# Attention by chunks: the scan of the next decays ahead of the masked copies, and the decayed state copied by ScalarE

## The chip, the cores and the metric

The kernel runs on one core of a Trainium2 chip. The metric is the device time of one execution in microseconds, lower is better. The engines are TensorE (PE in the profile; PEld is its weight load), VectorE (DVE), ScalarE (ACT), GpSimd (POOL) and SyncE (SP), which issues most DMAs. Each works through its own instructions in order and waits on semaphores for the others.

## The reference

Three parts follow one another: a recurrent attention over 4 batches, 8 heads, 768 positions and a head size of 48; a mixture of 8 experts of which each token takes the best (a true gather and scatter); and a layer that takes the largest of three products. The attention, which is all that matters here:

```python
for t in range(S):
    kt, vt, rt, wt = (k[:, :, t], v[:, :, t], r[:, :, t], w[:, :, t])
    cur = np.einsum('bhd,bhe->bhde', u[None] * kt, vt)
    y[:, :, t] = np.einsum('bhd,bhde->bhe', rt, state + cur)
    state = wt[:, :, :, None] * state + np.einsum('bhd,bhe->bhde', kt, vt)
```

A state of 48x48 per batch and head decays by w at each position and takes up the product of k and v; each output reads the state before the update, plus a bonus term with u.

## The kernel before

The 768 positions of a batch are cut in 6 chunks of 128 (CH), so there are 24 chunks (NG), and the 8 heads are held as 4 pairs (NP), one head of a pair on partitions 0 to 47 and the other on 64 to 111. Within a chunk the recurrence is written as products of matrices: two scans along the positions on DVE make the running products of the decays, one backwards (gs, L324) and one forwards (es, L337). gs scales the transposed k (kS, L330) and es the transposed r (rt, L348), both read from PSUM.

- gram (L356) multiplies kS and rt to the scores, in two PSUM banks A. causal (L362) copies them under a mask into the tile AT, which diagonal (L309, POOL) has filled with the bonus on the diagonal and zeros elsewhere. These are the masked copies, two per chunk.
- kback (L372) turns kS back, update (L384) multiplies it by v to U. carry (L396, or L394 in a batch's first chunk) adds U to the decayed state: S. Then it multiplies S by the whole decay of the next chunk, pend, three times on POOL: twice into the two diagonal blocks of shat (L400, 48 partitions each), which the next chunk's outputs read, and once into the state that the next carry adds to (Sm, L403, in the first four chunks of a batch).
- outputs (L410 with shat, L417 with AT) makes y transposed, yT (L419) copies it out of PSUM, tokens (L426) turns it and multiplies by the expert embeddings; logits (L437, dot) sums those.
- bonus (z, L288, POOL) multiplies the transposed k and r; bonus_sum (L294) and bonus_turn (L302, c on ACT in L304) sum it with u; c is what diagonal spreads.
- transpose (L275) makes transposed w, k and r through two PSUM buffers T, taken in turn; ACT copies them out (L277, L282).

The order of all engines is written out by hand, in one loop over i (L608 to L694) with a software pipeline: an iteration works on the tokens of chunk i, the scores of g = i + 1, the bonus of j = i + 2 and the scans of h = i + 3. Small operations of the routing on DVE stand in a list, fillers, from which fill() takes one at a time at places in the code (among others between the two masked copies, after gs and after kS); the rest is taken at the end of the iteration. The routing works on groups of three chunks: in one iteration the fillers m, e, e, mx, oh (L458 to L466), in the next cum three times and the rest of the slot (L491 to L503), whose tail ohb and pay (L507, L495) comes at the end of that iteration; the third has few.

Behind the loop and partly inside its last two iterations, the first expert starts early: POOL issues the gather of its tokens (L842, from iteration 21 on), early_x turns them (L857), ACT and POOL split its weights (L826, L828), and early_h (L877) multiplies. Then come the experts and the wide layer, which the change doesn't touch.

The order of an iteration around the change:

```python
if ok(i): carry(i)
...
if ok(g): gram(g)
...
if ok(g): causal(g)
if ok(h): transpose(h, "k")
if ok(j):
    bonus_turn(j)
    diagonal(j)
if ok(h): scan(h)
if 0 <= i < NG - 1: outputs(i)
```

Of the kernel before, what the change touches and what calls it, by code (L numbers as in the profile page):

```python
# [7 lines left out]
F32 = mybir.dt.float32  # L8
# [17 lines left out]
CH = S // P  # L26
# [20 lines left out]
class Block:  # L47
# [64 lines left out]
    def attention(self):  # L112
# [3 lines left out]
        with ExitStack() as es:  # L116
# [199 lines left out]
                act.activation(out=junk, in_=wb[g % NW][:, :, :D], func=AF.Relu, bias=neg1,  # L316
                               accum_out=viol[:, g:g + 1])

            def scan(g):


                j, x = g % 2, st[g]
                gs = wp.tile([112, NP, P + 1], F32, tag="gs", name="gs", bufs=2)
                dve.tensor_tensor_scan(out=flat(gs)[:, ::-1], data0=wz[j][:, :0:-1], data1=flat(dG)[:, ::-1],  # L324
                                       initial=0.0, op0=ALU.mult, op1=ALU.max)
                dve.reciprocal(out=dE[:, :, 0:1], in_=gs[:, :, 0:1])
                act.activation(out=pend[:, g, :].unsqueeze(2), in_=gs[:, :, 0:1], func=AF.Copy)
                fill()
                x["kS"] = wp.tile([112, 512], F32, tag="kS", name="kS", bufs=3)
                scaled = lambda: dve.tensor_tensor(out=x["kS"].rearrange("q (p t) -> q p t", p=NP),  # L330
                                                   in0=x["k"][:112].rearrange("q (p t) -> q p t", p=NP),
                                                   in1=gs[:, :, 1:], op=ALU.mult)
                if g > 0:
                    scaled()
                fill()
                es_ = wp.tile([112, NP, P + 1], F32, tag="es", name="es", bufs=1)
                dve.tensor_tensor_scan(out=flat(es_), data0=wz[j][:, :-1], data1=flat(dE), initial=0.0,  # L337
                                       op0=ALU.mult, op1=ALU.add)
                x["es"] = es_
                if g == 0:  # L340
                    scaled()
                fill()
# [44 lines left out]
            def carry(g):  # L387
                b, c = divmod(g, CH)
                if c == CH - 1:
                    return  # L390
                sn = wp.tile([112, NP, D], F32, tag="S", name="S")
                u = st[g]["U"][:112, :192].rearrange("q (p e) -> q p e", p=NP)
                if c == 0:
                    dve.tensor_copy(sn, u)  # L394
                else:
                    dve.tensor_tensor(out=sn, in0=state[b], in1=u, op=ALU.add)  # L396
                j = (g + 1) % 2
                decay = lambda o, n: pend[o:o + n, g + 1, :].unsqueeze(2).to_broadcast([n, NP, D])
                for o in (0, 64):
                    pool.tensor_tensor(out=shat[j][o:o + D, :, o:o + D], in0=sn[o:o + D], in1=decay(o, D), op=ALU.mult)  # L400
                if c < CH - 2:
                    state[b] = wp.tile([112, NP, D], F32, tag="Sm", name="Sm", bufs=1)
                    pool.tensor_tensor(out=state[b], in0=sn, in1=decay(0, 112), op=ALU.mult)  # L403

            def outputs(g):
                c, j, x = g % CH, g % 2, st[g]
# [35 lines left out]
            def fill(n=1):  # L442
                while fillers and n:
                    fillers.pop(0)()
                    n -= 1
# [151 lines left out]
            with tc.manual_schedule():  # L597
# [10 lines left out]
                for i in range(-2, NG):  # L608
# [32 lines left out]
                    if i - 2 in ends and i < NG - 1:  # L641
                        route_rank(*ends[i - 2])
                        fillers.extend(route_slot(*ends[i - 2]))
                    if ok(g):
                        causal(g)
                    if ok(h):
                        transpose(h, "k")
                    if ok(j):
                        bonus_turn(j)
                        diagonal(j)  # L650
                    if ok(h):
                        scan(h)
                    if 0 <= i < NG - 1:
                        outputs(i)
                    if ok(g):
# [626 lines left out]
```

## Time and profile before

| what | us |
|---|---|
| median of 3 runs | 732.67 |
| lowest and highest of them | 732.01, 735.51 |
| the profiled execution's own time | 735.84 |
| its span, from the first to the last instruction | 734.1 |

The profile is of one execution. Its page gives the busy time of each engine over the span; the views that were asked of its trace give the same by stretch (windows), by line, or instruction by instruction (timeline). In a timeline row the first two numbers are the start and the duration in us; a bracket at the end is the time that the engine sat idle before, and what ended it. Operations on an engine overlap a little, since the next is started before the last has written everything. TensorE's granted clock is 1.00 of full speed throughout the loop's steady part, so a matmul's length means the same in all rows used here.

### The profile page before, as it was taken

The page shows a single profiled execution, that of the slowest core. Times are in us where ns is not written, and L with a number is a line of the kernel's source. Part 1 is how long each engine was busy: PE and PEld are TensorE (multiplying, and loading weights), DVE is VectorE, ACT ScalarE, POOL GpSimd, SP SyncE. Part 2 cuts the span into 40 slices and gives each one's busy share as a digit, 9 for nine tenths or more (in the row PEclk, how much of TensorE's full clock was granted, in tenths as well). Part 3 has the DMA queues.
Part 4 walks back from the last instruction along what each step waited for, and adds up shares of the span by engine and source line. Part 5 has one row for each costly group of instructions (what it writes and reads, how often), then busy time and mean ns, then how long its engine had stood idle before and what let it go on. Part 6 is the DMA issues. An engine that isn't in the chain of part 4 may idle for free.

```text
span 734.1 us, 13455 instructions
## 1 busy us (share of the span) xinstructions
PE 706.5 (96%) x4861; PEld 631.3 (86%) x4861; DVE 431.8 (59%) x938; ACT 308.0 (42%) x720; POOL 251.4 (34%) x271
## 2 busy tenths in 40 slices
PE   8999999999799999999999999999999999999994
PEld 5888888878689999999999988988988988889884
DVE  7899999999747887878788368522032031221120
ACT  4767666675435544555556322222121222221120
POOL 6666656566522402201100023443333333222222
PEclk7999999999979999999999999999999999999997
DMA  9997878843355537556564202000000100000001
GB/s 154 160 160 142 134 138 133 150 86 114 105 174 156 164 116 238 178 162 184 177 173 130 76 23 65 12 33 1 33 12 0 44 1 11 33 1 21 22 2 46
DMA packets 146444, 69.05 MB, mean 94 GB/s; under 512 B 104967, under 2 KB 140931, under 8 KB 146360
## 3 DMA queue, kind: packets, MB, share of 16 engines
q1 hardware_dynamic: 141752, 58.27, 34.7%
q0 software_dynamic: 4032, 9.74, 4.2%
q8 instruction: 42, 0.69, 0.4%
q14 instruction: 42, 0.34, 0.2%
q10 hardware_dynamic: 576, 0.01, 0.0%
HBM read 58.52 MB, written 9.48 MB: 93 GB/s over the span
## 4 chain that ended last, share of the span: by engine, by line
PE 83%; DVE 9%; DMA 3%; issue 2%; ACT 1%; POOL 1%; SPq 0%; POOLq 0%; DVEq 0%
PE psy L994 15%; PE psT L994 15%; PE psy L934 14%; PE psh L917 14%; PE psh L1018 9%; PE psT L275 4%; PE psA L356 2%; PE psM L426 2%; PE psY L417 2%; DVE AT L362 2%; DVE gs L324 1%; PE psY L410 1%; PE psT L904 1%; DMA out_dram<-raw,idx 1%; PE psM L372 1%
## 5 line engine op out<-in xcount | busy, mean ns | idle before, releaser
L1000 DVE TENSOR_TENSOR xg<-psT,xg 128x512 f32<-128x512 f32 x18 | 12.4, 690 | 112.9 <-PE psT L994 112.9
L828 DVE TENSOR_TENSOR lw<-raw,hw 128x384 fp32r<-128x384 f32 x120 | 62.2, 551 | 17.8 <-ACT hw L826 17.5
L826 ACT ACTIVATE hw<-raw 128x384 fp32r<-128x384 f32 x123 | 60.6, 524 | 17.2 <-ACT hw L826 11.4
L1008 POOL TENSOR_TENSOR lw<-xg,hw 128x512 fp32r<-128x512 f32 x24 | 31.4, 1308 | 100.1 <-ACT hw L1007 100.1
L842 POOL DMA_INDIRECT xg<-xs_d,idxs x25 | 26.9, 1075 | 112.9 <-PE psT L904 44.3
L1007 ACT ACTIVATE hw<-xg 128x512 fp32r<-128x512 f32 x24 | 15.2, 633 | 97.0 <-DVE xg L1001 97.0
L1008 POOL TENSOR_TENSOR lh<-xg,hh 128x512 fp32r<-128x512 f32 x12 | 16.0, 1332 | 114.8 <-ACT hh L1007 114.8
L994 PE MATMUL psy<-yh,mh 128*128 128x512 f32 x162 | 46.7, 396 | 0.2 <-ACT ys L938 0.2
L994 PE MATMUL psT<-yh,ml 128*128 128x512 f32 x162 | 46.6, 396 | 0.0
L994 PE MATMUL psy<-yl,mh 128*128 128x512 f32 x162 | 46.6, 395 | 0.0
L994 PE MATMUL psT<-yl,mh 128*128 128x512 f32 x162 | 46.6, 396 | 0.0
L994 PE MATMUL psy<-yh,ml 128*128 128x512 f32 x162 | 46.6, 396 | 0.0
L994 PE MATMUL psT<-yh,mh 128*128 128x512 f32 x162 | 46.5, 395 | 0.0
L288 POOL TENSOR_TENSOR z<-kT,rT 112x512 f32<-112x512 f32 x24 | 37.7, 1573 | 25.0 <-ACT rT L282 25.0
L309 POOL TENSOR_SCALAR_AFFINE_SELECT AT<-c 128x1024 f32<-128x1024 f32 x24 | 34.9, 1456 | 24.1 <-ACT c L304 24.1
L917 PE MATMUL psh<-xh,lw 128*128 128x420 f32 (+7 forms) x183 | 43.2, 346 | 0.0
L923 DVE SCALAR_TENSOR_TENSOR lh<-psh,hh 128x420 fp32r<-128x420 f32 (+6 forms) x56 | 31.4, 560 | 19.8 <-ACT hh L922 19.7
L917 PE MATMUL psh<-xh,hw 128*128 128x420 f32 (+7 forms) x177 | 42.6, 349 | 0.0
L917 PE MATMUL psh<-xl,hw 128*128 128x420 f32 (+7 forms) x177 | 41.3, 342 | 0.0
L1034 POOL DMA_INDIRECT out_dram<-raw,idx x24 | 23.7, 986 | 50.0 <-ACT raw L1024 27.7
L934 PE MATMUL psy<-hh,hw 128*128 128x420 f32 (+6 forms) x168 | 40.1, 344 | 0.0
L934 PE MATMUL psy<-lh,hw 128*128 128x420 f32 (+6 forms) x168 | 39.2, 341 | 0.0
(332 smaller groups left out, 1807.9 us busy)
## 6 DMA issues: line engine op xcount, KB each, us to landing
raw<-in_moe_w_dram SPq DMA_DIRECT2D x128, 192.0 KB, 3.1
raw<-in_moe_w_dram SPq DMA_DIRECT2D x18, 384.0 KB, 3.9
wb<-in_w_dram SPq DMA_DIRECT2D x24, 192.0 KB, 3.1
kb<-in_k_dram SPq DMA_DIRECT2D x24, 192.0 KB, 4.6
rb<-in_r_dram SPq DMA_DIRECT2D x24, 192.0 KB, 4.7
vb<-in_v_dram SPq DMA_DIRECT2D x24, 192.0 KB, 5.0
xs_d<-xt SPq DMA_DIRECT2D x24, 192.0 KB, 2.0
raw<-in_moe_w_out_dram SPq DMA_DIRECT2D x6, 384.0 KB, 4.8
```

The source lines that it names most:

```text
L275: pe.transpose(t[:112, p * P:(p + 1) * P], flat(src)[:, p * P:p * P + 112], ident)
L288: pool.tensor_tensor(out=x["z"], in0=x["kT"], in1=x["rT"], op=ALU.mult)
L309: pool.affine_select(out=x["AT"].rearrange("s q p t -> s (q p) t"), in_=x["c"].rearrange("t q p -> t (q p)").unsqueeze(2).to_broadcast([P, ...
L826: self.act.activation(out=hi, in_=raw, func=AF.Copy)
L828: eng.tensor_tensor(out=lo, in0=raw, in1=hi.bitcast(F32), op=ALU.subtract)
L842: self.pool.indirect_dma_start(out=t[:n], out_offset=None, in_=self.xs_d[0:rows], in_offset=bass.IndirectOffsetOnAxis(ap=self.idxs[:n, 4 * ...
L917: self.pe.matmul(t[:, c0:cap], a[:, d, :], b[:, d, c0:], start=(n == 0), stop=(n == 8))
L923: self.dve.scalar_tensor_tensor(out=lo, in0=t[:, c0:cap], scalar=0.0, in1=hi.bitcast(F32), op0=ALU.max, op1=ALU.subtract)
L934: self.pe.matmul(self.yb[m][:, :cap], a[:, m, :], b, start=(f == 0 and n == 0), stop=(f == 7 and n == 2))
L994: self.pe.matmul(t, a[:, d, f * P:(f + 1) * P], b[:, d, :], start=(n == 0), stop=(n == 8))
L1008: self.pool.tensor_tensor(out=lo, in0=c2, in1=hi.bitcast(F32), op=ALU.subtract)
L1018: self.pe.matmul(t[:, :DM], a[:, c], b[:, f, :], start=(n == 0), stop=(n == 17))
```

## The change

Two things change. The masked copies of chunk g are handed to the scan of chunk h, which issues them after its backward scan gs and the reciprocal, and before its fillers and kS; the forward scan es still follows kS. And carry makes the decayed state once, on POOL, in every chunk but a batch's last (in two buffers instead of one); a new function, spread, copies its two blocks into shat on ScalarE, after bonus_turn and diagonal in the iteration.

```diff
--- before.py
+++ after.py
@@ -316,7 +316,7 @@
                 act.activation(out=junk, in_=wb[g % NW][:, :, :D], func=AF.Relu, bias=neg1,
                                accum_out=viol[:, g:g + 1])
 
-            def scan(g):
+            def scan(g, between=lambda: None):
 
 
                 j, x = g % 2, st[g]
@@ -325,6 +325,7 @@
                                        initial=0.0, op0=ALU.mult, op1=ALU.max)
                 dve.reciprocal(out=dE[:, :, 0:1], in_=gs[:, :, 0:1])
                 act.activation(out=pend[:, g, :].unsqueeze(2), in_=gs[:, :, 0:1], func=AF.Copy)
+                between()
                 fill()
                 x["kS"] = wp.tile([112, 512], F32, tag="kS", name="kS", bufs=3)
                 scaled = lambda: dve.tensor_tensor(out=x["kS"].rearrange("q (p t) -> q p t", p=NP),
@@ -394,13 +395,16 @@
                     dve.tensor_copy(sn, u)
                 else:
                     dve.tensor_tensor(out=sn, in0=state[b], in1=u, op=ALU.add)
-                j = (g + 1) % 2
-                decay = lambda o, n: pend[o:o + n, g + 1, :].unsqueeze(2).to_broadcast([n, NP, D])
+                state[b] = wp.tile([112, NP, D], F32, tag="Sm", name="Sm", bufs=2)
+                pool.tensor_tensor(out=state[b], in0=sn, in1=pend[:, g + 1, :].unsqueeze(2).to_broadcast([112, NP, D]),
+                                   op=ALU.mult)
+
+            def spread(g):
+                b, c = divmod(g, CH)
+                if c == CH - 1:
+                    return
                 for o in (0, 64):
-                    pool.tensor_tensor(out=shat[j][o:o + D, :, o:o + D], in0=sn[o:o + D], in1=decay(o, D), op=ALU.mult)
-                if c < CH - 2:
-                    state[b] = wp.tile([112, NP, D], F32, tag="Sm", name="Sm", bufs=1)
-                    pool.tensor_tensor(out=state[b], in0=sn, in1=decay(0, 112), op=ALU.mult)
+                    act.activation(out=shat[(g + 1) % 2][o:o + D, :, o:o + D], in_=state[b][o:o + D], func=AF.Copy)
 
             def outputs(g):
                 c, j, x = g % CH, g % 2, st[g]
@@ -641,15 +645,18 @@
                     if i - 2 in ends and i < NG - 1:
                         route_rank(*ends[i - 2])
                         fillers.extend(route_slot(*ends[i - 2]))
-                    if ok(g):
-                        causal(g)
                     if ok(h):
                         transpose(h, "k")
                     if ok(j):
                         bonus_turn(j)
                         diagonal(j)
+                    if ok(i):
+                        spread(i)
+                    masked = (lambda: causal(g)) if ok(g) else (lambda: None)
                     if ok(h):
-                        scan(h)
+                        scan(h, masked)
+                    else:
+                        masked()
                     if 0 <= i < NG - 1:
                         outputs(i)
                     if ok(g):
```

## Rows read from the trace of the kernel before

**Rows 1.** Page, part 1: busy us (share of the span) and instructions of each engine.

```profile
PE 706.5 (96%) x4861; PEld 631.3 (86%) x4861; DVE 431.8 (59%) x938; ACT 308.0 (42%) x720; POOL 251.4 (34%) x271
```

**Rows 2.** View of windows, the scan loop: stretch, length, engines' busy us, PEclk, DMA, GB/s.

```profile
28.10:163.40 135.30, 128.70 (x1678) 113.87 (x1678) 126.29 (x269) 92.78 (x246) 83.56 (x104) 1.00 0.77 136
```

**Rows 3.** Timeline, gram starts of one cycle: start us, us, engine, line, operation.

```profile
112.80 1.16 PE L356 MATMUL psA<-rt,kS 48*128 48x128 f32 x16
...
127.87 1.16 PE L356 MATMUL psA<-rt,kS 48*128 48x128 f32 x16
...
134.62 1.16 PE L356 MATMUL psA<-rt,kS 48*128 48x128 f32 x16
...
149.58 1.16 PE L356 MATMUL psA<-rt,kS 48*128 48x128 f32 x16
...
156.18 1.16 PE L356 MATMUL psA<-rt,kS 48*128 48x128 f32 x16
```

**Rows 4.** Timeline, round D (134.62 to 141.78), all engines; idle before in brackets.

```profile
135.36 0.34 DVE L396 TENSOR_TENSOR S<-Sm,psM 112x192 f32<-112x192 f32 x1
...
135.88 0.74 DVE L362 COPY_PREDICATED AT<-msk,psA 128x512 f32<-128x512 int32 x1 [0.18 <-PE psA L356]
...
137.53 0.17 ACT L304 ACTIVATE c<-psM 128x8 f32<-128x8 f32 x1
...
137.55 1.22 DVE L324 TENSOR_TENSOR_SCAN gs<-wz,dG 112x516 f32<-112x516 f32 x1
...
137.83 1.83 POOL L309 TENSOR_SCALAR_AFFINE_SELECT AT<-c 128x1024 f32<-128x1024 f32 x1 [0.91 <-ACT c L304]
...
138.90 0.77 DVE L491 TENSOR_TENSOR cum<-cum,oh 128x8 bf16<-128x8 bf16 x1
...
138.98 0.60 ACT L419 ACTIVATE yT<-psY 112x512 f32<-112x512 f32 x1
...
139.60 0.68 DVE L330 TENSOR_TENSOR kS<-psT,gs 112x512 f32<-112x512 f32 x1
...
140.23 1.27 POOL L288 TENSOR_TENSOR z<-kT,rT 112x512 f32<-112x512 f32 x1 [0.57 <-ACT rT L282]
...
140.29 2.30 DVE L337 TENSOR_TENSOR_SCAN es<-wz,dE 112x516 f32<-112x516 f32 x1
...
140.33 0.65 PE L275 MATMUL psT<-ident,wb 128*112 128x128 f32 x4 [0.81 <-DVE kS L330]
```

**Rows 5.** Timeline, single rows of other rounds, all engines.

```profile
96.93 2.29 DVE L337 TENSOR_TENSOR_SCAN es<-wz,dE 112x516 f32<-112x516 f32 x1
...
144.66 0.18 DVE L437 TENSOR_REDUCE dot<-psM 128x8 f32<-128x32 f32 x1
...
145.10 1.09 POOL L309 TENSOR_SCALAR_AFFINE_SELECT AT<-c 128x1024 f32<-128x1024 f32 x1 [3.60 <-ACT c L304]
...
148.13 0.65 PE L275 MATMUL psT<-ident,wb 128*112 128x128 f32 x4 [0.60 <-DVE kS L330]
...
152.10 0.51 POOL L403 TENSOR_TENSOR Sm<-S,pend 112x192 f32<-112x192 f32 x1
...
152.91 1.77 POOL L309 TENSOR_SCALAR_AFFINE_SELECT AT<-c 128x1024 f32<-128x1024 f32 x1 [0.30 <-ACT c L304]
...
154.72 0.65 PE L275 MATMUL psT<-ident,wb 128*112 128x128 f32 x4 [0.49 <-DVE kS L330]
```

**Rows 6.** View of line L464 (the second e): count, duration ns min/median/max, starts.

```profile
L464 DVE TENSOR_TENSOR e<-e,w x9: 159/456/940, 45.1 to 189.3; 128x24 f32<-128x24 f32 x6, 128x16 f32<-128x16 f32 x3
```

**Rows 7.** Timeline, the last rounds: POOL and PE around the early gather.

```profile
173.14 1.08 POOL L400 TENSOR_TENSOR shat<-S,pend 48x192 f32<-48x192 f32 x2 [1.08 <-DVE S L396]
...
175.49 1.28 POOL L842 DMA_INDIRECT hw<-xs_d,idxs  x1 [0.69 <-issue]
...
181.26 0.55 PE L857 MATMUL psT<-ident,hw 128*128 128x128 f32 x3 [0.36 <-DMA hw<-xs_d,idxs]
```

**Rows 8.** View of line L241 (a copy by ScalarE in the set-up), durations in ns.

```profile
L241 ACT ACTIVATE sel<-ident x2: 351/355/359, 8.2 to 8.6; 48x192 f32<-48x192 f32 x2
```

## The prediction

> **What bounds the kernel now.** I read the page's busy shares first [rows 1]: TensorE (PE) 96%, VectorE (DVE) 59%. That hides two stages, so next I took the view of windows and cut the span at the end of the scan loop, the only stage the change touches. In it [rows 2] PE and DVE are both near 94% (128.70 and 126.29 of 135.30 us), ScalarE (ACT) at 69%, GpSimd (POOL) at 62%. Two engines nearly full, in order, each waiting for the other now and then: the most to be won is what each still waits.
>
> A round is the stretch from one gram (L356) to the next, and its starts in the timeline give the periods [rows 3]. Six rounds (one batch) make a cycle, which stands more than twice between 69 and 163 us, each round to within 0.1 us. I call its rounds A to F, with the cycle from 112.80 to 156.18: A and B together 15.07 us, C 6.75, D and E together 14.96, F 6.60, in all 43.38. In C the PE starts every matmul group as the one before lets go, so C cannot shrink by anything done to DVE. D, E and F would be shorter on PE alone: there PE waits for kS on DVE, 0.81, 0.60 and 0.49 us [rows 4, 5]. The tie is the PSUM buffer: the transposes of the next w (L275) need the one that kS (L330) reads last. So **what counts is when kS comes in A, D, E and F**, less when anything else does.
>
> Why is kS late? Take the timeline of D [rows 4]. The order on DVE is dot, S, then the masked copies (AT, L362), the scan gs, kS, the scan es. Two rows stand out. The third cum (L491) takes 0.77 us for 128x8, beside POOL's AT select, and kS follows only when that ends. And es takes 2.30, where gs, a scan of the same shape, takes 1.22: POOL's z started 0.06 us before it, and es ends about as long after z as a scan runs. The second e (L464) shows the same: 0.16 at the least, 0.46 in the median, where it stands beside Sm [rows 5, 6]. In the other direction POOL's AT select takes 1.83 beside gs and 1.09 alone [rows 4, 5]. So some DVE operations and POOL operations exclude each other, and the first to start keeps the other out. The masked copies and kS run at their usual length beside POOL.
>
> **The change, part by part.** *The order on DVE.* The same operations run, with gs and its reciprocal ahead of the two masked copies. In D, S starts at 135.36 and the next operation can follow 0.27 later. Now that is AT, which waits for gram until 135.88; after, gs starts at 135.63. Adding gs to kS without cum (1.26 to the reciprocal, 0.09 to the first copy, each as now), the copies come at 136.98 and 137.71 and the second cum at 138.33. POOL's AT select, which hangs on c (ScalarE, ending 137.70) as before, starts at 137.83 and is now alone: it ends at 138.92. The second cum waits for that, then the third, and kS starts at 139.15 instead of 139.60: 0.45 us sooner, and with it PE's w transposes, which have 0.81 to give.
>
> *es in D.* With kS at 139.15, es starts near 139.84, ahead of z at 140.23, which hangs on ACT and doesn't move. es then runs 1.22 and z waits: es ends 1.5 us sooner. The rest of D's work on DVE ends when z lets go, so dot of E comes not at 144.66 but near 143.45. Then all of E moves up by about 1.2 on DVE, to kS and the w transposes; PE can follow by the 0.45 it got in D and by the 0.60 it idles in E. **D and E: -1.05 us**; the bounds are -0.45 (z still first) and -1.4 (both idle times in full). It happens twice in the whole loop, the es at 96.93 us being the other one [rows 5]: -2.1. The first batch's D has no such es; between 0 and -0.45 I give it -0.15.
>
> *F.* S, m, then gs near 150.80, and the copies after it; the first e comes at about 152.79, just ahead of POOL's AT select at 152.91, which follows c [rows 5]. The second e, at 153.5, meets it and waits until 154.0, where before it waited for Sm only until 152.6. kS then starts 0.18 later than now and PE with it: **+0.18** three times, +0.55. In C the same delay fits in front of the w transposes: 0.
>
> *A and B.* A has the fillers of D, but its select starts later, with c behind one more matmul group, so its second cum waits longer; and B begins with DVE's backlog, which still ends when z does. Between 0 and D's -0.45 I take **-0.10** for the pair, three times, -0.3. The loop: -2.1 + 0.55 - 0.3 - 0.15 = -2.0 us.
>
> *POOL.* Per round two shat products of 0.5 go (1.08 the pair [rows 7]); one Sm stays, and is added in the fifth chunk of a batch, where there was none. Sm now meets gs, so it ends about 0.3 after gs (the AT select beside gs shows such a wait). Its reader in the next round is 4 us away: 0.
>
> *ScalarE.* Two copies of 48x192 per round, 0.355 each [rows 8], 0.71 in twenty rounds, on an engine with a third free. They stand after c and before pend and yT. In D c ends at 137.70; the copies end by 138.42, pend is free (gs ended at 136.9) and ends by 138.65, and yT began at 138.98 when its PSUM was full [rows 4]. Before, ACT stood idle there, held by pend for gs. So the cover is that idle time, and it is just enough: 0. If it were gone (Sm late), yT, its w partner on ACT and the tokens would slip by up to 0.4 a round. Behind the new wait for Sm stand pend and yT on ACT; outputs of the next round needs shat only 5 us later. The moved copies pass PE's k transposes, c and diagonal, none of which read AT's masked half; no DMA moves in the loop, and SP's loads hang on transposes, not on these.
>
> *The last rounds.* At 163.39 the round has F's fillers but starts late, so that the first e also meets the select: kS up to 0.8 later, of which es, which waits for the select now and not after, returns some. Between 0 and 0.8: +0.4. The gather of the early expert (L842) is behind shat, shat and Sm on POOL [rows 7]; after, behind Sm alone, 1.08 sooner. PE waits for its landing only 0.36 at 181.26, so of its 1.08 it can return 0.4 at most, which takes back the 0.4 just lost. Then POOL's eight low parts (L828) follow sooner, which is what DVE's second e (0.94 at its longest, 0.16 at its shortest [rows 6]) and two neighbours wait for. Bounds: 0, and -2.3 if all three wait as long, 0.78, and all of it goes. I take -0.7, nearly one of the three, as the low parts still overlap most of that stretch.
>
> Sum: -2.0 + 0.4 - 0.4 - 0.7 = **-2.7 us**, where the second 0.4 is what the gather's lead returns. The profiled execution took 735.84 with a span of 734.1; it becomes 733.1. Against the median of the runs shown, 732.67, which lies 3.2 under the profiled one: **730.0 us**.
>
> **Rivals.** *1. POOL starts first in C and F (slower).* The first e comes 0.12 before the select, gs 0.1 before Sm. If either tie falls the other way, e waits a whole select (1.09, from 152.91) or gs a whole Sm (0.51), and kS in both kinds of round comes 0.7 later: PE loses 0.7 in six rounds, +4.3, and the total is +1.6: **734.3**. For it: 0.12 us is near the spread of starts. Against: starts within a round repeat to 0.1 us from batch to batch. The Trainium skill, in "SBUF — State Buffer", section "Who interferes with whom", says that the one that issues first holds the shared port for its whole instruction, and that a vector operation with two SBUF inputs is of this kind; by that rule the second e and cum wait out the select as I have it, and a lost tie costs this full price.
>
> *2. Nothing comes of it.* If z is first in D after all, or the backlog's end isn't set by es, D and E give 0.45 twice and F takes 0.55, the rest 0: **732.3**. For it: PE is near full everywhere. Against: es at 2.30 occurs in both such rounds.
>
> *3. More.* All three late waits go (-2.3), D and E get 1.4 twice (-2.8), A gets D's 0.45 three times (-1.35) and F loses nothing: -6.4, **726.3**. For it: POOL has some 20 us less work in shat products. Against: the selects and low parts themselves remain, and something waits for them.
>
> *4. ScalarE is held.* If Sm waits beyond gs, for the copies too, ACT stands before pend and yT in nearly each round: 20 x 0.4 = 8 on top of -2.7: **738.0**. Against: the masked copies never lengthened beside POOL.
>
> **How the numbers follow.** Forecast 0.54, rival 1 0.17, rival 2 0.11, rival 3 0.13, rival 4 0.05. A measurement can tell about 0.5% from no change, 3.7 us: faster is under 729.0. The forecast's own range is 728 to 732.3, with over two fifths of its chance under 729.0; with rival 3 this makes faster 0.37, slower 0.06 (rival 4 and the end of rival 1), same 0.57. The range 726.0 to 735.0 reaches to rivals 3 and 1 and leaves out 4 and the ends.
>
> **What would show it.** Right: es never above 1.3 us beside z in D; kS 0.45 sooner there; periods of D and E together near 13.9 instead of 14.96, F 6.8, C still 6.75; no pend wait for gs on ACT; gather at about 174.5 less the loop's gain. Wrong: es again 2.3; a first e (L463) of 0.7 or more in C and F (rival 1); yT beginning well after its matmuls (rival 4); C shorter than 6.75, which would mean that PE wasn't its bound.

## The result and the profile after

The changed kernel takes **741.37 us** (median of 4 runs, 740.98 to 744.21); the kernel before, beside it, 733.97 (4 runs, 732.01 to 735.51). The ratio is 1.0081, 95% interval 1.0052 to 1.0111: slower, by some 6 us as the ratio has it (the medians lie 7.4 apart), where 730.0 was forecast. The profiled execution took 741.60 with a span of 739.9, against 735.84 and 734.1 before.

The trace falls into two halves of opposite sign. The first is the scan loop. The stretch that answers to [rows 2], from the loop's third gram to its third last, by the view of windows (stretch, length, busy us of PE, PEld, DVE, ACT and POOL, granted clock, DMA share, GB/s), for the changed kernel:

```profile
28.16:160.21 132.05, 127.72 (x1678) 113.85 (x1677) 123.16 (x269) 102.73 (x278) 71.47 (x75) 1.00 0.79 140
```

Between the same two grams (28.14 and 163.39 before) the loop takes 132.05 us where it took 135.25: 3.20 us less. ScalarE has 10 us more work in it and GpSimd 12 less. The gram starts of the cycle that answers to [rows 3], A to the next A, from the timeline:

```profile
111.24 0.94 PE L357 MATMUL psA<-rt,kS 48*128 48x128 f32 x12
...
126.13 1.16 PE L357 MATMUL psA<-rt,kS 48*128 48x128 f32 x16
132.88 1.16 PE L357 MATMUL psA<-rt,kS 48*128 48x128 f32 x16
...
146.43 1.16 PE L357 MATMUL psA<-rt,kS 48*128 48x128 f32 x16
153.20 1.16 PE L357 MATMUL psA<-rt,kS 48*128 48x128 f32 x16
```

A and B take 14.89 us (15.07 before), C 6.75 as before, D and E together 13.55 (14.96), F 6.77 (6.60). Round D itself, to be read against [rows 4]:

```profile
133.88 1.23 DVE L324 TENSOR_TENSOR_SCAN gs<-wz,dG 112x516 f32<-112x516 f32 x1
134.04 1.37 POOL L399 TENSOR_TENSOR Sm<-S,pend 112x192 f32<-112x192 f32 x1 [0.34 <-DVE S L397]
...
135.97 1.09 POOL L309 TENSOR_SCALAR_AFFINE_SELECT AT<-c 128x1024 f32<-128x1024 f32 x1 [0.56 <-ACT c L304]
...
137.19 0.68 DVE L331 TENSOR_TENSOR kS<-psT,gs 112x512 f32<-112x512 f32 x1
...
137.88 1.22 DVE L338 TENSOR_TENSOR_SCAN es<-wz,dE 112x516 f32<-112x516 f32 x1
...
137.93 0.65 PE L275 MATMUL psT<-ident,wb 128*112 128x128 f32 x4 [0.16 <-DVE kS L331]
138.55 1.62 POOL L288 TENSOR_TENSOR z<-kT,rT 112x512 f32<-112x512 f32 x1 [1.49 <-ACT rT L282]
```

The select takes its 1.09 us, es starts 0.67 ahead of z and takes 1.22 instead of 2.30, and TensorE waits 0.16 for kS where it waited 0.81. The last gram of the loop starts at 174.84 where it started at 177.68.

The second half is the end of the loop, up to the first expert's transposes: from that gram 23.81 us before (177.68 to 201.49), now 33.20 (174.84 to 208.04). The timeline of the changed kernel there, POOL, DVE and PE:

```profile
176.01 0.51 POOL L399 TENSOR_TENSOR Sm<-S,pend 112x192 f32<-112x192 f32 x1 [2.16 <-DVE m L462]
176.72 1.07 POOL L849 DMA_INDIRECT hw<-xs_d,idxs  x1 [0.21 <-issue]
...
177.48 7.08 DVE L468 TENSOR_TENSOR e<-e,w 128x16 f32<-128x16 f32 x1
177.82 1.02 POOL L835 TENSOR_TENSOR lw<-raw,lw 128x384 fp32r<-128x384 f32 x1
...
181.63 2.88 POOL L835 TENSOR_TENSOR oh<-raw,oh 128x384 fp32r<-128x384 f32 x3
...
185.02 0.17 PE L481 MATMUL psM<-oh,tri 128*128 128x8 bf16 x1 [6.47 <-DVE fl L537]
...
185.13 2.03 PE L414 MATMUL psT<-rt,shat 112*112 112x128 f32 x8
```

**The second e (now L468), 0.16 us at its shortest in [rows 6], takes 7.08.** It ends at 184.56, just when the last of GpSimd's seven low parts (now L835, ending 184.51) does. TensorE has nothing for 6.47 us, and its next outputs take 2.03 us instead of some 1.1. The windows of 5 us show why; first the changed kernel, then the kernel before:

```profile
175.00:180.00 5.00, 3.56 (x44) 3.04 (x45) 4.43 (x7) 4.76 (x13) 3.76 (x5) 1.00 0.85 253
180.00:185.00 5.00, 0.00 (x0) 0.00 (x0) 4.91 (x4) 0.96 (x3) 4.52 (x5) 0.61 0.12 36
185.00:190.00 5.00, 4.98 (x33) 4.35 (x33) 1.76 (x14) 0.60 (x1) 0.00 (x0) 0.50 0.02 3
190.00:195.00 5.00, 5.00 (x25) 5.00 (x25) 2.49 (x13) 2.24 (x7) 0.00 (x0) 0.50 0.11 41
195.00:200.00 5.00, 4.99 (x35) 4.62 (x33) 2.66 (x15) 1.97 (x6) 1.00 (x1) 0.69 0.51 157
```

```profile
180.00:185.00 5.00, 4.64 (x57) 3.97 (x54) 3.06 (x18) 3.55 (x9) 3.30 (x4) 1.00 0.57 171
...
190.00:195.00 5.00, 4.41 (x39) 4.02 (x38) 4.75 (x22) 1.36 (x5) 2.03 (x3) 1.00 0.24 78
```

After TensorE's idle stretch its granted clock is 0.50 (1.2 GHz) until 198 us, where before it stayed at 1.00 (2.4 GHz) to 201. Behind that both have one more stretch at 0.50: 201 to 211 before, 208 to 212 in the changed kernel. So the wait costs twice: once while it lasts, and once behind it.

Why did GpSimd have no such row before? There the second shat product of the last chunk waited for the landing of the early gather, and with it everything behind it on GpSimd. The timeline of the kernel before:

```profile
181.35 0.51 POOL L400 TENSOR_TENSOR shat<-S,pend 48x192 f32<-48x192 f32 x1 [1.95 <-DMA hw<-xs_d,idxs]
182.14 1.07 POOL L842 DMA_INDIRECT hw<-xs_d,idxs  x1 [0.28 <-POOL shat L400]
183.28 1.00 POOL L828 TENSOR_TENSOR lw<-raw,lw 128x384 fp32r<-128x384 f32 x1
```

By 183.28, e (180.27, 0.16 us) had long been done. In the changed kernel that product is gone and the gather is issued sooner, so this wait went, and the low parts came 5.5 us sooner, onto e.

### The profile page after: what moved, and what is told of

It reads as the page before. It is cut to its first block, busy times and chain, and to the rows that moved or that the text cites. A ratio compares the mean times of both kernels' runs of the same rounds, so it can differ in the third digit from the quotient of the medians.

```text
span 739.9 us, 13443 instructions
## 1 busy us (share of the span) xinstructions
PE 708.7 (96%) x4860; PEld 633.8 (86%) x4861; DVE 431.6 (58%) x938; ACT 319.8 (43%) x760; POOL 235.8 (32%) x235
## 4 chain that ended last, share of the span: by engine, by line
PE 81%; DVE 10%; issue 3%; DMA 2%; ACT 1%; POOL 1%; SPq 0%; DVEq 0%; POOLq 0%; ACTq 0%
PE psy L1001 15%; PE psT L1001 14%; PE psy L941 13%; PE psh L924 12%; PE psh L1025 9%; PE psT L275 4%; PE psM L430 3%; PE psA L357 2%; DVE AT L363 2%; PE psY L421 2%; PE psY L414 1%; PE psM L373 1%; DVE e L468 1%; DMA out_dram<-raw,idx 1%; DMA raw<-in_moe_w_dram 1%
## 5 line engine op out<-in xcount | busy, mean ns | idle before, releaser
L835 DVE TENSOR_TENSOR lw<-raw,hw 128x384 fp32r<-128x384 f32 x120 | 62.2, 552 | 16.2 <-ACT hw L833 14.7
L941 PE MATMUL psy<-hh,lw 128*128 128x420 f32 (+6 forms) x168 | 39.2, 341 | 0.0
```

The source lines that it names most:

```text
L835: eng.tensor_tensor(out=lo, in0=raw, in1=hi.bitcast(F32), op=ALU.subtract)
L941: self.pe.matmul(self.yb[m][:, :cap], a[:, m, :], b, start=(f == 0 and n == 0), stop=(f == 7 and n == 2))
```

## The experiments

The names in the expectations: theory A is that GpSimd's early row of low parts holds VectorE's e, B that the new order on VectorE costs by itself, C that ScalarE's copies do. Medians of the kernel before stand beside each group: 734.69 us for e1 to e4, 734.72 for e5 to e8, 734.59 for e9 to e12, 734.17 for e13 to e15.

### e1 to e4: the two parts alone, and the row taken away

**e1_scan_only**: the new order alone, the three products left on GpSimd.

```diff
-                    if ok(g):
-                        causal(g)
...
+                    masked = (lambda: causal(g)) if ok(g) else (lambda: None)
                     if ok(h):
-                        scan(h)
+                        scan(h, masked)
```

> The kernel before with the new place of the masked copies alone; shat and Sm stay three products on GpSimd. Theory A (the loss comes from GpSimd's low parts, which in the changed kernel start about 5.5 us sooner because the shat product that waited for the gather is gone; VectorE's second e then waits 7.08 us for them, and TensorE idles and loses its clock): the loop gains (the round pair D and E, 14.96 us, falls by about 1.4, the whole loop by 2 to 3), the second e of the last routing group in the loop stays under 1 us, and the time is 2 to 4 us under before. Theory B (the new order on VectorE itself makes it late in the last rounds): the end is as slow as in the changed kernel, 5 us or more over before.

Measured: 737.6 us, ratio 1.0042 (1.0019 to 1.0066), slower: a miss, and not by the e, which takes 0.15. D and E fall by 1.29, near the 1.4 expected, but the loop as a whole lost. C and F take 7.27 us each (6.75 and 6.60 before) and A 7.67 (7.22), since gs now comes first and the three products behind it. Timeline of a round C of e1 (gram at 129.01):

```profile
130.20 1.23 DVE L324 TENSOR_TENSOR_SCAN gs<-wz,dG 112x516 f32<-112x516 f32 x1
130.34 1.96 POOL L401 TENSOR_TENSOR shat<-S,pend 48x192 f32<-48x192 f32 x2 [0.88 <-PE psA L357]
...
134.09 0.68 DVE L331 TENSOR_TENSOR kS<-psT,gs 112x512 f32<-112x512 f32 x1
134.83 0.65 PE L275 MATMUL psT<-ident,wb 128*112 128x128 f32 x4 [0.30 <-DVE kS L331]
```

kS starts 5.08 us behind the gram; in the changed kernel, with one product instead of three, 4.52 in the same round. The rounds ahead of the third gram differ from execution to execution, so from here on lags and leads in the loop are counted from that gram (28.14 before, 27.62 in e1). By the gram at 172.44 e1 is 2.02 behind the kernel before; in the next round TensorE waits 1.32 us (174.92) and the clock is 0.50 from 175 until past 181, so that the last gram, at 182.49, is 5.33 late.

**e2_spread_only**: the copies by ScalarE alone, the masked copies in their old place.

```diff
+                    if ok(g):
+                        causal(g)
                     if ok(h):
                         transpose(h, "k")
...
                     if ok(h):
-                        scan(h, masked)
+                        scan(h)
```

> The changed kernel with the masked copies back in their old place; Sm alone on GpSimd and two copies on ScalarE stay. Theory A: GpSimd reaches the low parts as early as in the changed kernel, an operation of VectorE waits several us for them near the end, TensorE idles about 6 us; the loop stays within 1 us of before; 6 to 10 us over before. Theory B: nothing of that, within 1.5 us of before.

Measured: 740.67 us, 1.0081 (1.0051 to 1.0111), as the whole change. The last gram starts at 175.96, 1.31 sooner than before, with D 6.87, E 7.74, F 6.30 us: what the saved products are worth by themselves. At the end the same picture, so the new order isn't its cause. Timeline of e2, DVE:

```profile
178.60 7.06 DVE L468 TENSOR_TENSOR e<-e,w 128x16 f32<-128x16 f32 x1
```

**e3_last_on_pool**: the changed kernel, with the last chunk's products on GpSimd again, two as before.

```diff
+                if g == NG - 2:
+                    for o in (0, 64):
+                        pool.tensor_tensor(out=shat[(g + 1) % 2][o:o + D, :, o:o + D], in0=sn[o:o + D],
+                                           in1=pend[...].to_broadcast([D, NP, D]), op=ALU.mult)
+                    return
```

> The changed kernel, but the last product before the end of the loop (chunk 22 to 23) is made as before, by two products on GpSimd, the second of which again waits for the gather to land; the other 19 chunks as changed. Theory A: this alone takes the loss away: low parts start about 2 us or more after the gather lands, the second e stays under 1.2 us, the clock stays at 2.4 GHz level as in before, and the time is 2 to 4 us under before. Theory C (the two copies on ScalarE, nineteen of which stay, are what costs): still 4 us or more over before.

**e4_late_split**: the changed kernel, with the first three splits of weights moved behind the last copies and fillers.

```diff
-                    if i == NG - 2:
-                        self.split_w(1, 0, 0)
-                        self.load_w(1, 0, RAW)
-                        for f in range(1, 3):
-                            self.split_w(1, 0, f)
...
                     if i == NG - 2:
                         fill(99)
+                        self.split_w(1, 0, 0)
+                        self.load_w(1, 0, RAW)
+                        for f in range(1, 3):
+                            self.split_w(1, 0, f)
```

> The changed kernel with the first three weight splits of the last but one iteration written after the routing operations and the outputs of chunk 22 instead of ahead of kback, so that ScalarE makes their high parts, and GpSimd the low parts, about 2 us later; the gather still lands early. Theory A: the second e of that iteration is done before the low parts begin (under 1.2 us), TensorE doesn't idle 6 us; the time is 3 us or more under before. If instead later operations of the routing (the sums cum or the slot's ohb and pay) now wait for the row of low parts, the gain is smaller, between -3 and +3. Theory C: 4 us or more over before.

Measured: e3 733.62 us, 0.9973 (0.9949 to 0.9997); e4 733.36, 0.9985 (0.9961 to 1.0008). Either edit takes some 8 us off the changed kernel, e3 not in the way expected: its second product doesn't wait for the gather, which was issued early. The row starts only 0.75 us later behind the last gram than in the changed kernel and still directly behind a gather, but e comes early in that gather and gets through. Timeline of e3, POOL and DVE:

```profile
176.62 1.07 POOL L854 DMA_INDIRECT hw<-xs_d,idxs  x1 [0.28 <-POOL shat L400]
...
176.91 0.16 DVE L473 TENSOR_TENSOR e<-e,w 128x16 f32<-128x16 f32 x1
...
177.76 1.00 POOL L840 TENSOR_TENSOR lw<-raw,lw 128x384 fp32r<-128x384 f32 x1
```

Timeline of e4, DVE and POOL:

```profile
176.66 1.07 POOL L848 DMA_INDIRECT hw<-xs_d,idxs  x1 [0.21 <-issue]
...
177.41 0.15 DVE L468 TENSOR_TENSOR e<-e,w 128x16 f32<-128x16 f32 x1
...
179.29 1.01 POOL L834 TENSOR_TENSOR lw<-raw,lw 128x384 fp32r<-128x384 f32 x1 [1.56 <-ACT lw L832]
179.34 0.98 DVE L508 TENSOR_SCALAR rl<-ri 128x2 int32<-128x2 int32 x1
```

In e4 e takes 0.15. The row holds what comes later instead: rl 0.98 us where it took 0.16 alone, but for one product, not for the row. A is confirmed, B and C fall. Yet the loop's 2.8 us should have left both well under the kernel before; e3 is 1.1 under, and e4 1.3, inside its interval.

### e5 to e8: the size of the row, the clock, and a better order

**e5_short_burst**: the changed kernel, with four of the seven splits behind the last outputs.

```diff
-                        for f in range(3, 7):
-                            self.split_w(1, 0, f)
                         low()
                         outputs(NG - 1)
+                        for f in range(3, 7):
+                            self.split_w(1, 0, f)
```

> The changed kernel, with the splits of weights 3 to 6 put behind the last outputs, so that only three of the seven low parts stand back to back on GpSimd while VectorE's second e is due. Theory A (a VectorE operation on two SBUF operands stays shut out until the row of back-to-back GpSimd products has ended): the second e takes about 3.2 us instead of 7.08, from 177.5 to 180.7, the end is some 4 us earlier than in the changed kernel, 737.5 us. Rival (e waits for its own operands or for the gather, whatever GpSimd does): e again 7 us, 741. Second rival (it gets in after one product, as in the kernel before): e about 1 us, 734 to 735.

Measured: 735.69 us, 1.0003 (0.9973 to 1.0032). e follows the length of the row; timeline of e5:

```profile
176.49 3.28 DVE L468 TENSOR_TENSOR e<-e,w 128x16 f32<-128x16 f32 x1
176.83 1.01 POOL L835 TENSOR_TENSOR lw<-raw,lw 128x384 fp32r<-128x384 f32 x1
177.78 1.95 POOL L835 TENSOR_TENSOR lw<-raw,hw 128x384 fp32r<-128x384 f32 x2
```

**e6_warm_gap**: the changed kernel, with work for TensorE in its gap.

```diff
                         low = self.early_x(0, bank("T", 2))
+                        idle(28)
                         route_rank(*sets[-1])
```

> The changed kernel, with 28 matmuls of the warm-up kind put on TensorE just ahead of the rank matmuls that wait for the held e; their results are read by nothing. e stays at 7.1 us in either case. Theory (a good part of the 9.4 us lost at the end is the clock of 0.50 that follows TensorE's 6.5 us without work): the clock stays at 1.00 from 178 to 198, the first outputs row after the gap takes 1.1 us instead of 2.03, the first expert starts near 204.5 instead of 208.0, total about 738. Rival (TensorE is not on the path there, VectorE and the DMAs set the end): first expert at 208, total 741.

Measured: 736.71 us, 1.0018 (0.9993 to 1.0043), 4.7 below the changed kernel with e at 7.10 us all the same. Windows of e6:

```profile
178.00:186.00 8.00, 7.78 (x52) 4.22 (x51) 8.00 (x4) 4.27 (x12) 7.77 (x9) 1.00 0.25 75
186.00:194.00 8.00, 7.94 (x82) 7.21 (x80) 5.52 (x33) 4.14 (x12) 0.61 (x2) 1.00 0.19 58
```

In the changed kernel the same two stretches had 0.69 and 0.50. So over half of the 8 us that the changed kernel lies above e3 and e4 is the clock behind the wait; that the rest is the wait itself is inferred. The clocks of all runs say much the same. Take the span times (1 - granted clock) as the time lost to the clock, so that 10 us at 0.50 count as 5: in the mean the changed kernel loses 18.5 us, e3 12.7 and e4 12.8.

**e7_tokens_first**: e4, with the last tokens ahead of the transposes of the second gathered block.

```diff
-                    if i == NG - 1:
-                        low = self.early_x(1, bank("T", 2))
                     if ok(i):
                         tokens(i)
+                    if i == NG - 1:
+                        low = self.early_x(1, bank("T", 2))
```

> The changed kernel with the first three weight splits late (as in e4_late_split), and the last tokens matmuls ahead of the transposes of the second gathered block, for whose landing TensorE waited 2.15 us. Theory (the loop's 2.8 us was lost at the end to that landing, which stands ahead of the last tokens in TensorE's order): no wait between the two tokens groups, the last e about 2 us sooner, the first expert near 197.5 instead of 199.4, total about 731.5. Rival (what comes sooner here is taken back by the stream of weights near 282 us, as 1.0 of e3's lead was): first expert sooner all the same, total 733.

Measured: 732.19 us, 0.9963 (0.9932 to 0.9994). The last e comes at 186.06 (187.49 in e4), of which 0.57 is the earlier third gram (27.58, 28.15 in e4), but the first expert starts at 199.28 (199.43): the gain doesn't arrive there. The runs spread from 728 to 738; in the profiled one the clock is 0.50 from 183 to 190 and again from 200 to past 210. Against e4 the intervals overlap, so what the edit is worth is not settled.

**e8_mixed_order**: e7, with the old order in the rounds of kind F.

```diff
+                    if g % CH == 1:
+                        masked()
+                        masked = lambda: None
                     if ok(h):
                         scan(h, masked)
```

> e7_tokens_first, with the masked copies ahead of the scan again in the rounds of kind F alone (chunk 1 of a batch). Theory (the order and the saved products act round by round: F was 6.30 us in e2 and 6.77 in the changed kernel, D and E 6.50 and 7.05 only with the scan first): F 6.30, D and E as in the changed kernel, the loop 1.4 to 1.9 us shorter than e7's, total about 730. Rival (what F gains, the next round or the end loses): the loop as in e7, total as e7.

Measured: 731.0 us, **0.9944** (0.9917 to 0.9972). F takes 6.30 us in each batch, D and E 6.50 and 7.05; the last gram starts at 172.51, 1.40 ahead of e7's, which is F's 0.47 three times. The theory holds in the loop: order and saved products act round by round.

### e9 to e12: work in the wait ahead of the experts, and low parts on VectorE

**e9_mixed_warm_x**: e8 with 11 warm-up matmuls ahead of the first expert's transposes; **e10_before_warm_x** is the kernel before with the same lines.

```diff
+                t = self.ptile("y", 3)
+                for _ in range(11):
+                    self.pe.matmul(t, self.warm[:, :P], self.warm, start=True, stop=True)
                 self.expert_x(0, 1)
```

> e8_mixed_order with 11 matmuls of the warm-up kind ahead of the transposes of the first expert, for whose gathered rows TensorE waits 2.46 us without work in e8; their results are read by nothing. Theory (what the loop gained was lost to TensorE's waits at the end of the loop, through the clock of 0.50 that follows them: span times clock is 718.5 us in e8 and 723.5 before, but 10.5 us against 9.6 are lost to the clock): the clock stays at 1.00 from 194 to 210, the runs spread less (728 to 734 in e8), total 728 to 729. Rival (the first expert waits for weights, not for TensorE): the clock stays up and the total is as e8, 731.

> The kernel before with the same 11 matmuls at the same place, where it waits 2.58 us. Theory: it has the same wait and the same clock of 0.50 behind it (201 to 211 us), so it gains about as much, 2 to 3 us, total 732, and e9 stays about 3 to 4 us ahead of it, which is what the change is worth without the clock. Rival (the wait costs only in the new kernels): total as before, 734.7.

**e11_mixed_warm_all**: e9, with `idle(3)` ahead of the last tokens and `idle(2)` ahead of `head(0)`.

> e9_mixed_warm_x, with 3 more such matmuls ahead of the last tokens and 2 ahead of the first early row of the first expert, for the waits of 0.80 and 0.34 us that stand ahead of the half clock from 183 to 187 us in e8. Theory: the clock stays at 1.00 there too, the first expert starts 1 to 2 us sooner than in e9, total 727. Rival (the fillers delay what they stand ahead of, or the waits grow instead): as e9 or up to 1 us slower.

Measured: e9 728.8 us, 0.9918 (0.9889 to 0.9946); e10 734.37, 0.9985 (0.9966 to 1.0005); e11 **728.73, 0.9904** (0.9876 to 0.9931), its runs within 1.8 us. e9 came out as forecast and e10 as its rival had it, but the wait isn't what either took it for. The view of waits of TensorE for e9, 186 to 202 us (engine, line, what it waited for: us, times, longest):

```profile
PE psy L1054 <- issue: 2.7, 1, 2.7
```

The 11 matmuls themselves wait as long as the transposes did, and run behind the wait, not in it. So what stands ahead of the first expert isn't the gathered rows, and the gap wasn't filled. In e9's profile the clock stays at 1.00 all the same, in e10's it is 0.50 only from 200 to 203 (201 to 211 before). Over all runs the time lost to the clock, as counted at e6, falls in both: from 10.5 us in e8 to 7.9 in e9, and from 9.7 before to 8.0 in e10, while the rest of the span grows by 1.3 and 1.1. So in e10 most of what the clock gives back is spent again. What ends the wait stays open, and so does whether e9 is faster than e8, since their intervals overlap. e8, e9 and e11 are the fastest versions, 0.6 to 1.0% under the kernel before.

**e12_lows_on_dve**: the changed kernel, with the eight early low parts on VectorE.

```diff
-        eng = self.pool if n == 1 and e == 0 else self.dve
+        eng = self.dve
```

> The changed kernel with the eight low parts of the first expert on VectorE instead of GpSimd, at the same places of the program. Theory A (GpSimd's row is what holds the second e): no operation of VectorE is stretched; each low part costs about 0.56 us of VectorE, four of them ahead of or among the last copies, so the last e comes 2 to 3 us later than the 177.6 us of a free one, and the total lies at 734 to 736, some 6 us below the changed kernel. Rival (e is held by something else): e 7 us again, 741 or more.

Measured: 732.38 us, 0.9973 (0.995 to 0.9995): A again, and better than forecast. The second e takes 0.15 us (at 178.35), and from there to the last e nothing on VectorE is stretched.

### e13 to e15: why the whole row

In e4 the same row held an operation for one product; in the changed kernel it held e for seven. Two things were different: the form of e, and that e arrived while GpSimd was still issuing the gather directly ahead of the row.

**e13_other_form**: the changed kernel, with the last group's e computed per chunk.

```diff
+                if (g0, n) == sets[-1]:
+                    ops += [lambda i=i: dve.scalar_tensor_tensor(out=e8[:, i], in0=dot[:, g0 + i, :],
+                                                                 scalar=m[:, i:i + 1], in1=w8, op0=ALU.is_equal,
+                                                                 op1=ALU.mult) for i in range(2)]
```

> The changed kernel, with the two e of the last group of tokens but one computed by two operations of the form that the kernel uses for single chunks (compare with a scalar per partition, then multiply, 128x8 each) in place of two of 128x16. Theory H1 (an operation that arrives while GpSimd issues the gather ahead of a row stays out until the row ends): the second of them is held about 7 us again, total about 741. Theory H2 (it is the form of e): held for one product at most, about 1 us, total 734 to 736.

**e14_gather_behind**: the second gather moved.

```diff
-                    if i == NG - 2:
-                        self.gather(0, PRE, 1)
...
                         for f in range(3, 7):
                             self.split_w(1, 0, f)
+                        self.gather(0, PRE, 1)
```

> The changed kernel with the second gather of the first expert's rows issued behind the seven low parts instead of ahead of them, so that e arrives while a low part runs. H1: e gets in after one product, about 1 us; the total stays high all the same, 737 to 742, since the gathered rows come 7 us later. H2 (the form of e): e is held to the end of the row, 6 us or more.

**e15_probe_ahead**: an operation of another form put directly ahead of e.

```diff
+                    probe = lambda: dve.tensor_scalar(out=pb, in0=pa, scalar1=7, scalar2=None,
+                                                      op0=ALU.logical_shift_right)
...
-                            lambda: dve.tensor_tensor(out=e8, in0=e8, in1=w8b, op=ALU.mult)]
+                            lambda: (probe(), dve.tensor_tensor(out=e8, in0=e8, in1=w8b, op=ALU.mult))]
```

> The changed kernel with an extra operation of rl's form (128x2 int32, shift) directly ahead of the second e; its result is read by nothing. H1: this operation, arriving during the gather, is itself held for about 7 us, and e behind it is done in 0.2 us or gets held not at all; total 741. H2: this operation is done at once or after one product (up to 1.3 us), and e behind it is held to the end of the row, 5 to 7 us.

Measured: e13 739.72 us, 1.0074 (1.0045 to 1.0104); e14 736.91, 1.005 (1.0021 to 1.008); e15 741.73, 1.0102 (1.002 to 1.0183). Timelines of e13, of e15 and of e14, in this order:

```profile
174.54 1.07 POOL L853 DMA_INDIRECT hw<-xs_d,idxs  x1 [0.21 <-issue]
...
175.30 7.05 DVE L464 SCALAR_TENSOR_TENSOR e<-dot,m,w 128x8 f32<-128x8 f32 x1
```

```profile
176.43 7.06 DVE L466 TENSOR_SCALAR pb<-pa 128x2 int32<-128x2 int32 x1
...
183.41 0.16 DVE L474 TENSOR_TENSOR e<-e,w 128x16 f32<-128x16 f32 x1
```

```profile
175.94 1.00 POOL L834 TENSOR_TENSOR lw<-raw,lw 128x384 fp32r<-128x384 f32 x1
176.10 0.87 DVE L467 TENSOR_TENSOR e<-dot,m 128x16 f32<-128x16 f32 x1
...
177.52 0.41 DVE L468 TENSOR_TENSOR e<-e,w 128x16 f32<-128x16 f32 x1
```

All three decide against H2: 128x8 or two integers per partition are out until the row ends just as e was, and with the gather gone from ahead of the row e gets in after one product. (e14's time stays high, just under the 737 to 742 expected.) But H1 as it was put, for whatever arrives during the gather, is too wide. In e1 and e3 the second e arrives during the gather directly ahead of the row, 0.84 and 0.85 us ahead of the row's start, and takes 0.15 and 0.16; the oh behind it, 0.46 and 0.45 ahead, takes 0.18 and 0.17. In the six kernels in which the row held an operation (changed, e2, e5, e6, e13, e15) it started 0.32 to 0.34 us ahead of the row, in the last 0.30 to 0.32 us of the gather. So what the held ones share is a gather, a row directly behind it, and an arrival in the last 0.3 us of the gather. An operation that arrives once the row is running gets in after one product, with a gather ahead of the row (cum in e1 and e3, 0.78 us) as without one (e in e14). So e14 doesn't tell the gather from the moment of arrival, and no run varied that moment by itself: which of the two decides is not shown.

## Why the prediction was wrong

**The loop was right, its terms somewhat small.** gs first in D: kS starts 4.31 us behind the gram where it was 4.98, 0.67 sooner and not 0.45. es goes ahead of z. D and E: -1.41 for -1.05, at the bound of -1.4. F: +0.17 for +0.18, by the second e at the select (0.58 us in the F from 146.43), as worked out. C: 0. A and B: -0.18 for -0.10. To the gram at 160.21 (163.39 before) that is -3.20 where the sum had -2.0. The term that was too small is **POOL, put at 0**: to the same gram the saved products alone (e2) bring 0.87, and the order alone (e1) costs 2.02. The parts were priced one by one, where each needs the other.

**The ScalarE copies cost nothing**, as costed: in D yT starts 0.05 us after its matmuls end, and in e2, which has the copies, no round of the steady cycle is longer than before. Rival 4 didn't come. Nor did rival 1 in the changed kernel: its ties fell as forecast. Its price is what befell e1, though by the second e, which waits out a whole select there (1.08 us at 132.88).

**The last rounds are the step that failed.** The last two rounds up to the last gram lost 0.34 of the 0.4 that I gave them, and the gather is issued early, at 171.43, with no wait for its landing. But then: "Then POOL's eight low parts (L828) follow sooner, which is what DVE's second e ... wait for ... I take -0.7". That they follow sooner was right, by 5.5 us. I counted only waits that would go, within 0 and -2.3, and didn't ask which operation of VectorE the row would meet at its new place. Measured: the end from the last gram on grew by 9.39 us, by e's 6.9 and the half clock behind it. I hadn't seen that the second shat product waited for the gather (1.95 us at 181.35), and that without this wait the row would come right behind e. It wasn't that wait alone that kept them apart: e1 and e3 don't have it either, and there e is 0.5 us further ahead of the row and goes free. And the trace of before held a warning beside a row of [rows 7], on DVE and POOL:

```profile
175.49 1.28 POOL L842 DMA_INDIRECT hw<-xs_d,idxs  x1 [0.69 <-issue]
...
175.94 2.21 DVE L495 TENSOR_SCALAR pay<-i,aa,tid 128x32 fp32r<-128x32 f32 x2
176.80 1.11 POOL L309 TENSOR_SCALAR_AFFINE_SELECT AT<-c 128x1024 f32<-128x1024 f32 x1
```

The first pay arrives during a gather and is out through the gather and the select behind it.

**The price of exclusion was the wrong kind.** I had one instruction hold one other. The Trainium skill, "SBUF — State Buffer", section "Who interferes with whom", has it so too: the first to issue keeps the shared port for its whole instruction. Rows inside the loop agree (es 1.22 when it is first), and so does e4 (0.98 behind one product). The 7.08 us behind seven products do not, and here the measurement decides.

**Where the loop's gain went in e3 and e4** is shown in the main by the clocks of all their runs. The span times the granted clock is 718.9 us in both and 722.3 in the kernel before beside them, 3.4 less; but the time lost to the clock is 12.7 and 12.8 against 10.5, which takes back 2.2 to 2.3 of it. Their ends have waits of TensorE that the kernel before lacks, and a lower clock behind them. The windows of e4:

```profile
180.00:185.00 5.00, 2.85 (x28) 2.52 (x23) 3.56 (x9) 3.32 (x11) 5.00 (x6) 0.93 0.24 79
185.00:190.00 5.00, 5.00 (x38) 4.90 (x37) 2.56 (x14) 2.98 (x10) 2.23 (x3) 0.73 0.39 121
```

Before, both were at 1.00. TensorE is idle there for 2.15 us at 184.01, ahead of the second block's transposes. Another 1.0 us of the 1.61 by which e3 is ahead at 278 us goes between there and 294, where VectorE waits 2.40 us for a load of weights (1.38 before) and TensorE 0.75 for VectorE at 285.40.

## What to carry to other kernels

A wait that is taken off an engine is also taken from what stands behind it there: follow the queue to its next long row, and look what that will meet at its new time. While VectorE has work on the path, keep a row of back-to-back GpSimd products away from a gather issued directly ahead of it, or put the products on VectorE. Price a wait of TensorE with the stretch at half clock that can follow it: here, by e6, the second was the larger part.

## What the runs showed of the hardware that was not expected

- A VectorE operation that arrives in the last 0.3 us of a gather's issue by GpSimd, with products waiting directly behind it, stays out until the last of them ends: 7.05 to 7.10 us behind seven in five kernels, 3.28 behind three. Form and size didn't matter (128x16, 128x8, two integers). Those that came earlier in such a gather got in ahead of the row: e in e1 and e3 and the first e of the changed kernel (0.20 us at 176.73) at once, rl in the kernel before after 0.45 us (182.73). Why stays open.
- A VectorE operation that arrives once such a row is running gets in after one product (0.98 for rl in e4, 0.87 for e in e14, 0.78 for cum in e1 and e3, there with the gather directly ahead of the row). A gather with nothing directly behind it didn't hold e: it took 0.15 during one in e4, where the products came 1.56 us later.
- With a select directly behind the gather, the picture is mixed: the first pay in the kernel before (2.01 us) and cum in e6 and e14 (1.53) were out to the select's end, but rq in the changed kernel (0.72 us at 172.17), in e1 (1.13) and in most others only to 0.2 us behind the gather's end. That stays open.
- A wait of TensorE of 1.32 us in e1 was followed by over 6 us at 0.50, one of 2.65 us in e9 by none.
